# Folding layer 2's column DFT a second time, with the symmetry tests redistributed

## The chip, the cores and the metric

The kernel runs on one core of a Trainium2 chip. The metric is the device time of one execution in microseconds (us), lower is better; a kernel's time is the median of its runs.

The names of the engines: PE is TensorE (matrix products; PEld its weight loads), DVE is VectorE, ACT is ScalarE, POOL is GpSimd, and SP is the sync engine, which here issues nearly all DMAs. Each engine executes its own queue in order.

## The reference

```python
def _A_ref(x, dft_seq_re, dft_seq_im, dft_hid_re, dft_hid_im):
    a = jnp.einsum("bsd,ed->bse", x, dft_hid_re)
    b = jnp.einsum("bsd,ed->bse", x, dft_hid_im)
    return jnp.einsum("ts,bse->bte", dft_seq_re, a) - jnp.einsum("ts,bse->bte", dft_seq_im, b)

def _B_ref(x, w_gate, w_up, w_down):
    h = _sigmoid(jnp.einsum("bsd,df->bsf", x, w_gate)) * jnp.einsum("bsd,df->bsf", x, w_up)
    return jnp.einsum("bsf,fd->bsd", h, w_down)

x = x + _A_ref(_layernorm(x), ...)
x = x + _B_ref(_layernorm(x), ...)
x = x + _A_ref(_layernorm(x), ...)
x = x + _B_ref(_layernorm(x), ...)
```

x has 2048 rows of 640 columns, F is 1728, all float32. The DFT matrices (2048 x 2048 and 640 x 640, real and imaginary) are inputs. `_A_ref` is the real part of a two-dimensional DFT.

## The kernel before

**Numbers.** Float32 operands are split into two float16 parts, and a product is three matmuls: high by high, high by low, low by high (`PASSES`). A split is one ACT instruction (high, L237) and one DVE instruction (low, L239).

**Symmetries.** Cosine and sine rows repeat under t to S - t, S/2 - t, and d to 640 - d. So rows of x are folded in groups GA to GD, columns d with 640 - d: `fold_columns` (L593, L594) makes 321 even sums (EC) and 320 odd differences (EH), `fold_rows` scales and combines (L636 to L642), `fold_join` combines GA with GC (L675) and splits (L677, L682). Whether the input matrices do have these symmetries is tested on the chip while the layers run: a test loads rows or columns of a matrix with DMAs into a "room" of SBUF (L1502, L1519, L1562, L1571), DVE adds or subtracts mirrored parts in place (`test_rows` L1509 and L1511, `test_cols` L1525 to L1528, `test_hidden_rows` L1566, `test_hidden_cols` L1575), and ACT squares and sums the rest (L1481). If the sum is not tiny, a general path runs after the fast one. There are 100 tests and three rooms; a test's load is issued two tests ahead of its check. The list `spans` spreads the tests over the program by weights, 0.4 to 1.1 per unit of PE's time.

**The stages of a layer.** The DFT: `sequence(i, tp)` (L796) multiplies block i of folded rows (four blocks of 128) with the sequence matrix for even (EV) or odd (OD) outputs; `evict_sums` brings the sums from PSUM to SBUF in two halves (L237, L239) as operands z; `hidden(q, ph)` multiplies z with the hidden matrices, `product` (L922) going over three pieces of 128, 128 and 65 rows, for real and imaginary: 18 matmuls of 321 columns into two banks. `hidden_middle` does it for the middle row. `evict_hidden` copies the two banks out: on ACT alone (L971), or for q = 0 one half on ACT (L961) and sum and difference on DVE (L966). `join_hidden` (L996), `add_hidden` (L1009), the row statistics (L424 on DVE, L437 and L438 on ACT), `norm_apply` (L451, L453) and `norm_parts` (L463, L465) make normalized rows, `transpose_pe` (L540) and `transposed` (L550, L552) turn them, and the gate stage starts with `gate_up` (L1130). Later rows are turned by DMA transpositions (`pair_transpose`, L533). The gate stage goes on with `seven` and `four` (L1174: six steps of 54 products of 512 columns in all per column tile j; `snap` L1178 copies a running sum out on ACT between two steps), and the down stage is `stage` (L1430, L1411) or `down` (L1316), with `rows_add` (L1304) on DVE behind each step.

**The order of the work.** Layer 1's DFT follows a list written by hand (`OPENING`). From there, `steps` is the list of PE's work; every other piece of work is put before a step, by `when` (a time on a scale made of the steps' assumed durations) or by `run` (a step's number). A DVE, ACT, POOL or SP instruction therefore stands in its engine's queue at the place where its job comes in this order, and waits there. PSUM has eight banks, which are given out in the order in which they were freed. SBUF is cut into slots whose places are a table (`PLACES`). Layer 2's DFT starts at step `he`: its `order` list names 17 steps, and `run(he + n, ...)` puts the evictions and the row work between them. Its block 3 is joined by the job at `end + 3`, three units into the first step; blocks 0 and 1 are folded during layer 1's second gate stage and spilled, block 2 during its down stage. The split hidden matrices are kept in DRAM from layer 1 (`keep` in `drop_hidden`) and loaded again (`load_wh_again`, L907).

```python
for h in range(2):
    for j in range(0 if h else JC, NF):
        p = seven(j)
        steps += p[:4] + ([four(j - 1)] if j > (0 if h else JC) else []) + p[4:]
```

## Time and profile before

| | us |
|---|---|
| median of 3 runs | 1105.36 |
| lowest, highest | 1103.85, 1106.36 |
| the profiled execution | 1106.03 |
| its span, first to last instruction | 1104.2 |
| PE busy in the span | 1084.0 |
| DVE, ACT, POOL busy | 830.2, 572.9, 154.6 |

On a row of the profile stand the line of the kernel, the engine, the operation, what it writes and reads (`big` is the SBUF tile in which all slots lie, `acc` the PSUM banks), how often, the busy time, and in brackets the idle time of the engine before it with what ended that. The stages on PE by the trace: layer 1's DFT and its first gate products until 154, gate stage 154 to 243, down 243 to 332, gate 332 to 492, down 492 to 572; layer 2's DFT 572 to 612, gate 612 to 780, down 780 to 860, gate 860 to 1018, down to the end.

### The profile page before, as it was taken

The page shows a single profiled execution, that of the slowest core. Times are in us where ns is not written, and L with a number is a line of the kernel's source. Part 1 is how long each engine was busy: PE and PEld are TensorE (multiplying, and loading weights), DVE is VectorE, ACT ScalarE, POOL GpSimd, SP SyncE. Part 2 cuts the span into 40 slices and gives each one's busy share as a digit, 9 for nine tenths or more (in the row PEclk, how much of TensorE's full clock was granted, in tenths as well). Part 3 has the DMA queues.
Part 4 walks back from the last instruction along what each step waited for, and adds up shares of the span by engine and source line. Part 5 has one row for each costly group of instructions (what it writes and reads, how often), then busy time and mean ns, then how long its engine had stood idle before and what let it go on. Part 6 is the DMA issues. An engine that isn't in the chain of part 4 may idle for free.

```text
span 1104.2 us, 17528 instructions
## 1 busy us (share of the span) xinstructions
PE 1084.0 (98%) x6289; PEld 626.3 (57%) x6289; DVE 830.2 (75%) x1608; ACT 572.9 (52%) x1109; POOL 154.6 (14%) x250
## 2 busy tenths in 40 slices
PE   6999999999999999999999999999999999999997
PEld 3776444457774444457777844444677444444775
DVE  8996789868448999769887569895895356777962
ACT  7776547765315665555225544476761345555520
POOL 3110153312333151000110100012000010000010
PEclk9999999999999999999999999999999999999999
DMA  8414765366996877756742058645569856666521
GB/s 273 155 61 71 199 184 203 115 193 191 251 249 233 251 250 202 235 174 214 229 141 73 1 62 194 200 154 182 185 163 177 265 180 208 202 196 194 190 88 64
DMA packets 183079, 194.70 MB, mean 176 GB/s; under 512 B 76451, under 2 KB 145474, under 8 KB 182982
## 3 DMA queue, kind: packets, MB, share of 16 engines
q1 hardware_dynamic: 182342, 190.87, 58.8%
q0 software_dynamic: 640, 2.62, 0.6%
q8 instruction: 51, 0.84, 0.3%
q14 instruction: 46, 0.38, 0.1%
HBM read 145.29 MB, written 31.91 MB: 160 GB/s over the span
## 4 chain that ended last, share of the span: by engine, by line
PE 87%; DVE 8%; issue 2%; DMA 1%; ACT 1%; POOL 0%; SPq 0%; DVEq 0%; POOLq 0%; ACTq 0%
PE acc L1174 36%; PE acc L1430 17%; PE acc L1130 14%; PE acc L1316 8%; PE acc L922 4%; PE acc L1411 2%; PE acc L1283 2%; PE acc L834 2%; DVE big L642 1%; DMA big<-big 1%; DVE quad L424 1%; DVE big L239 1%; PE acc L796 1%; DVE big L1509 1%; DVE big L594 0%
## 5 line engine op out<-in xcount | busy, mean ns | idle before, releaser
L1174 PE MATMUL acc<-big 128*128 128x512 f16 x2160 | 467.8, 379 | 2.8 <-ACT big L1178 1.9
L1174 PEld LDWEIGHTS <-big 128*128 128x128 f16 x2160 | 211.3, 98 | 257.8 <-issue 3.5
L1430 PE MATMUL acc<-big 128*128 128x320 f16 x1512 | 213.2, 299 | 0.4 <-DVE big L1304 0.4
L1178 ACT ACTIVATE big<-acc 128x512 f32<-128x512 f32 x160 | 94.0, 593 | 191.9 <-PE acc L1174 167.5
L1430 PEld LDWEIGHTS <-big 128*128 128x128 f16 x1512 | 147.9, 98 | 58.5 <-issue 0.6
L1130 PE MATMUL acc<-big 128*128 128x512 f16 (+1 forms) x900 | 156.6, 336 | 0.0
L1130 PEld LDWEIGHTS <-big 128*128 128x128 f16 x900 | 87.9, 98 | 67.7 <-DVE big L239 0.2
L1481 ACT ACTIVATE big<-big 128x768 f32<-128x768 f32 (+6 forms) x106 | 79.0, 745 | 53.2 <-DVE big L1511 17.0
L1304 DVE SCALAR_TENSOR_TENSOR big<-acc,big 128x320 f32<-128x320 f32 x112 | 53.1, 485 | 53.7 <-PE acc L1411 27.2
L239 DVE SCALAR_TENSOR_TENSOR big<-big 128x640 f16<-128x640 f32 (+7 forms) x94 | 75.9, 830 | 22.5 <-ACT big L237 19.4
L1316 PE MATMUL acc<-big 128*128 128x320 f16 x656 | 89.3, 299 | 0.0
L1391 DVE TENSOR_TENSOR big<-big 128x512 f16<-128x512 f32 x126 | 85.3, 688 | 2.3 <-ACT big L1390 2.3
L1390 ACT ACTIVATE big<-big 128x512 f16<-128x512 f32 x126 | 74.0, 618 | 25.0 <-DVE big L1391 11.1
L237 ACT ACTIVATE big<-big 128x640 f16<-128x640 f32 (+9 forms) x94 | 63.8, 707 | 35.7 <-POOL big L1082 15.8
L1316 PEld LDWEIGHTS <-big 128*128 128x128 f16 x656 | 64.2, 98 | 25.1
L1224 DVE TENSOR_TENSOR big<-big,acc 128x512 f32<-128x512 f32 x40 | 27.3, 682 | 44.4 <-PE acc L1174 30.6
L516 ACT ACTIVATE big<-big 128x384 f16<-128x384 f32 (+2 forms) x56 | 36.0, 667 | 36.6 <-DVE big L501 17.2
L1181 ACT ACTIVATE big<-big 128x512 f32<-128x512 f32 x80 | 49.7, 622 | 9.7 <-DVE big L1224 6.6
L386 POOL DMA_INDIRECT out<-big,rows x8 | 8.6, 1070 | 310.9 <-DVE big L1304 173.5
L1509 DVE TENSOR_TENSOR big<-big 128x512 f32<-128x512 f32 x64 | 46.2, 722 | 5.9 <-DMA big<-in_ct 5.7
L1402 DVE TENSOR_TENSOR big<-big 128x512 f32<-128x512 f32 x72 | 50.1, 697 | 0.1
L439 POOL TENSOR_SCALAR rowt<-rowt 128x1 f32<-128x1 f32 x24 | 13.0, 540 | 242.4 <-ACT big L437 242.4
(199 smaller groups left out, 1230.2 us busy)
## 6 DMA issues: line engine op xcount, KB each, us to landing
big<-in_ct SPq DMA_DIRECT2D x256, 128.0 KB
big<-kept_f SPq DMA_DIRECT2D x63, 320.0 KB
big<-kept_S SPq DMA_DIRECT2D x33, 512.0 KB
big<-kept_w SPq DMA_DIRECT2D x33, 320.0 KB
big<-in_ct SPq DMA_DIRECT2D x32, 256.0 KB
big<-kept_G SPq DMA_DIRECT2D x21, 320.0 KB
kept_S<-big SPq DMA_DIRECT2D x13, 512.0 KB
big<-in_wg SPq DMA_DIRECT2D x19, 320.0 KB
```

Of the source, the lines that this page charges most:

```text
L237: nc.scalar.activation(dh, src, AF.Copy, scale=s)
L239: nc.vector.scalar_tensor_tensor(dl, src, s, dh, op0=OP.mult, op1=OP.subtract)
L1130: nc.tensor.matmul(ps, w[wp][:, d * P : (d + 1) * P], xt[:, xp, :], start=(d == 0 and wp == HI and xp == HI), stop=(d == ND - 1 and wp == LO))
L1174: nc.tensor.matmul(ps, wt, xt, start=start and n == 0, stop=n == len(todo) - 1, skip_group_check=not start)
L1178: nc.scalar.activation(dst, ps, AF.Copy)
L1304: nc.vector.scalar_tensor_tensor(xe, ps[:, :EH], CB, xe, op0=OP.mult, op1=OP.add)
L1316: nc.tensor.matmul(held["pd", i, e][0][:, :EH], held["t", half, j].parts[hp][:, i * P : (i + 1) * P], held["w", 2, j].parts[wp][:, e * EH ...
L1390: nc.scalar.activation(h, v, AF.Copy)
L1391: nc.vector.tensor_tensor(l, v, h, op=OP.subtract)
L1430: nc.tensor.matmul(ps[:, :EH], a[n][hp][:, i * P : (i + 1) * P], w[n][:, wp], start=fresh and m == 0, stop=m == len(todo) - 1, skip_group_ ...
L1481: nc.scalar.activation(v, v, AF.Square, accum_out=new_sum()[:p])
L1509: nc.vector.tensor_tensor(bd[:, :, 1], bd[:, :, 0], bd[:, :, 1], op=same)
```

## The change

**The second fold.** In layer 2 the 321 even sums and the 320 odd differences are folded again, d with 320 - d: 161 sums and 160 differences each (`fold_again`, four new DVE instructions for a parity pair). Even outputs of the hidden DFT then need only one of the two and odd outputs the other. `product` writes even outputs to the first 161 columns of the bank and odd ones to the next 161; the first two pieces of d have 161 columns each, and the third, with rest rows of both kinds (33 + 32), has 322. So 12 of the 18 matmuls of a `hidden` have half the columns. The evictions put the outputs back in turn: they read the bank with `"p (h k) -> p k h"`. The doubled first column moves to the front of the folded tile. The hidden matrices for layer 2 are loaded raw by `load_wh2` and split by `split_wh2` during layer 1's second down stage, in place of the stores and reloads of the split ones. Scales XF and ZS are halved.

**The order of layer 2's DFT.** `sequence(3, EV)` comes before `sequence(2, OD)`, and both q = 0 steps come together ahead of `sequence(3, OD)`. Block 3 is joined after `evict_sums(0, EV, 0)`, first for EV and, two evictions later, for OD. Products by TensorE, with weight loads between; ahead of them stands the last sequence step. Before:

```order
L796 LDWEIGHTS big
L796 MATMUL acc_312<-big 65x256
L922 LDWEIGHTS big
L922 MATMUL acc_315<-big 128x321
L922 LDWEIGHTS big
L922 MATMUL acc_315<-big 128x321
```

After, at the fifth product of `hidden(0, 0)`:

```order
L976 LDWEIGHTS big
L976 MATMUL acc_327<-big 128x161
L976 LDWEIGHTS big
L976 MATMUL acc_327<-big 128x161
L976 LDWEIGHTS big
L976 MATMUL acc_327<-big 128x322
L976 LDWEIGHTS big
```

Where nine products of 321 columns went into a bank, six of 161 do, and then three of 322.

DVE's queue at the start of layer 2's DFT, from the end of block 3's `fold_rows`. Before (L675 and L682 are `fold_join`, L239 is an eviction, L966 is `evict_hidden`):

```order
L642 SCALAR_TENSOR_TENSOR big<-big,quad_77 128x320
L675 TENSOR_TENSOR big<-big 128x321 x2
L675 TENSOR_TENSOR big<-big 128x320 x2
L682 TENSOR_TENSOR big<-big 128x2x321
L682 TENSOR_TENSOR big<-big 128x2x320
L239 SCALAR_TENSOR_TENSOR big<-acc_314,big 128x512
```

After (L699 and L708 are `fold_join`, L684 is `fold_again`, L241 an eviction):

```order
L656 SCALAR_TENSOR_TENSOR big<-big,quad_78 128x320
L241 SCALAR_TENSOR_TENSOR big<-acc_326,big 128x512
L699 TENSOR_TENSOR big<-big 128x321 x2
L699 TENSOR_TENSOR big<-big 128x320 x2
L684 TENSOR_TENSOR big<-big 128x161
L684 TENSOR_TENSOR big<-big 128x160
L684 TENSOR_TENSOR big<-big 128x161
L684 TENSOR_TENSOR big<-big 128x160
L708 TENSOR_TENSOR big<-big 128x321 x2
L241 SCALAR_TENSOR_TENSOR big<-acc_66,big 128x512
```

An eviction moved ahead of the join, and four instructions came in between join and split; the other two evictions, four more second folds and the splits of the OD half follow.

**The tests.** Six tests of the second fold's symmetry are new (`test_hidden_fold`), 106 in all. The weights in `spans` are new; the hidden tests get a room of their own and one test more of time between load and check. By DVE's rows, layer 1's second down stage has 5 tests after 9, layer 2's first gate stage 27 after 24 (with `gate_up`), its first down stage 4 after 6, its last gate stage 49 after 33, and its last down stage 5 after 5. SP's queue in layer 2's last gate stage, between two loads of a `kept_S` weight (L1104 before, L1167 after). Before:

```order
L1104 DMA big<-kept_S_2853 128x2048
L1109 DMA big<-kept_w_4_1115 128x2x384
L1502 DMA big<-in_ct 128x1x256 x8
L1103 DMA big<-kept_w_5_1151 128x1280
L1104 DMA big<-kept_S_2936 128x2048
```

After:

```order
L1167 DMA big<-kept_S_2868 128x2048
L1172 DMA big<-kept_w_4_1115 128x2x384
L1565 DMA big<-in_ct 128x1x256 x12
L1625 DMA big<-in_wh 128x1x320 x2
L1565 DMA big<-in_ct 128x1x256 x4
L1166 DMA big<-kept_w_5_1151 128x1280
L1167 DMA big<-kept_S_2951 128x2048
```

Eighteen loads of tests stand between the weights where eight stood.

**Else.** Layer 2's rows for the second half are prepared at 6, 18, 42 and 51 units of its first down stage instead of 6, 20, 46 and 56. At the start eleven small DVE instructions make the scales `hs2` behind `hs`. The slots are placed anew. The diff, cut to its core:

```diff
-XF = 2.0**8
+XF = 2.0**7
...
+    hs2 = pool.tile([P, 5], F32, name="hs2")
...
+        p = part[:, 34:35]
+        nc.vector.tensor_scalar(hs2[:, 0:1], p, 1.0, 0.5 * CS, op0=OP.is_ge, op1=OP.mult)
+        nc.vector.tensor_scalar(hs2[:, 0:1], hs2[:, 0:1], 0.5 * CS, None, op0=OP.add)
+        for k, op, a, b in ((1, OP.is_le, 31, 32), (2, OP.is_ge, 33, 34), (3, OP.is_le, 30, 31), (4, OP.is_ge, 33, 33)):
+            for c, v in ((hs2[:, k : k + 1], a), (part[:, 36 + k : 37 + k], b)):
+                nc.vector.tensor_scalar(c, p, float(v), 0.5 * CS, op0=op, op1=OP.mult)
+        nc.vector.tensor_tensor(hs2[:, 1:5], hs2[:, 1:5], part[:, 37:41], op=OP.add)
...
+    def fold_again(to, f, r):
+
+        c, every = EH - 2 * r, (slice(None),) * (len(f.shape) - 1)
+        for n, to_c, op in ((HE + 1, 0, OP.add), (HE, HE + 1, OP.subtract)):
+            nc.vector.tensor_tensor(to[(*every, slice(to_c, to_c + n))], f[(*every, slice(0, n))],
+                                    f[(*every, slice(c, c - n, -1))], op=op)
...
             if 1 in do:
-                nc.scalar.activation(take_parts(key, i)[:, :, 0, :w], f[:, GB::2], AF.Copy)
-                if n:
-                    nc.gpsimd.memset(take_parts(key, i)[:, :, :, EH : EH + 1], 0.0)
+                fold_again(a, b, n)
             if 2 in do:
-                p = take_parts(key, i)
-                nc.vector.tensor_tensor(p[:, :, 1, :w], f[:, GB::2], p[:, :, 0, :w], op=OP.subtract)
-                folded_at[fold, i] = True
+                nc.scalar.activation(p[:, :, 0, :EC], a, AF.Copy)
+            if 3 in do:
+                nc.vector.tensor_tensor(p[:, :, 1, :EC], a, p[:, :, 0, :EC], op=OP.subtract)
...
     def product(ps, ph, r, at, m):
-        for d, (_, n) in enumerate(KT[r]):
-            w = held["h", r, d].f16[:n]
+        for d, (_, n) in enumerate(KT):
+            o = ps[:m, : EC + 1 if steps else EC]
+            if steps and d < 2:
+                c = (r + d) % 2
+                o = ps[:m, c * (HE + 1) : (c + 1) * (HE + 1)]
+            ws = [w[:n, : o.shape[1]] for w in held["h", r, d].parts]
...
-                    nc.tensor.matmul(ps[:m, :EC], z[:, at : at + m], w[:, 384 * wp : 384 * wp + EC],
+                    nc.tensor.matmul(o, z[:, at : at + m], ws[wp],
...
+    def sums_of_bank(ps):
+        return ps[:, : EC + 1].rearrange("p (h k) -> p k h", h=2) if steps else ps[:, :EC]
+
+    def in_order(v):
+        return v.rearrange("p (k h) -> p k h", h=2) if steps else v[:, :EC]
...
-                nc.scalar.activation(v[:, n], ps[:, :EC], AF.Copy, scale=CY)
+                nc.scalar.activation(in_order(v[:, n]), sums_of_bank(ps), AF.Copy, scale=CY)
...
-                     (sequence, 2, OD), (hidden, 0, 0), (sequence, 3, EV), (hidden, 1, 0), (sequence, 3, OD),
-                     (hidden, 0, 1), (hidden, 2, 0), (hidden, 3, 0), (hidden, 1, 1), (hidden, 2, 1), (hidden, 3, 1),
-                     (hidden_middle,)]
+                     (sequence, 3, EV), (sequence, 2, OD), (hidden, 0, 0), (hidden, 0, 1), (sequence, 3, OD),
+                     (hidden, 1, 0), (hidden, 1, 1), (hidden, 2, 0), (hidden, 3, 0), (hidden_middle,),
+                     (hidden, 2, 1), (hidden, 3, 1)]
...
-            u = d0 + ((2, 20, 47, 57) if first else (6, 20, 46, 56))[i]
+            u = d0 + ((2, 20, 47, 57) if first else (6, 18, 42, 51))[i]
...
-    spans = [(start_of(0, "d", 0) + 6, start_of(0, "d", 0) + 38, 0.4), (start_of(0, "d", 0) + 76, start_of(0, "e"), 0.55),
...
+    spans = [(d[0] + 6, d[0] + 38, 0.5), (d[0] + 76, d[1] - 43, 0.12), (d[1] - 43, d[1] - 3, 0.7), (d[1] - 3, d[1] + 57, 0.3),
+             (c - 11, j, 0.8), (j, d2 - 28, 0.6), (d2 - 28, d2 - 4, 0.8), (d2 + 6, d2 + 38, 0.35), (j2, j2 + 23, 0.5),
+             (j2 + 23, j2 + 63, 1.4), (j2 + 63, e2, 1.1), (e2, e2 + 25, 0.6)]
```

184 lines of the change are left out of this document (118 added, 66 removed), and 64 rows, old and new, of the table PLACES.

## The prediction

> **What bounds the kernel now.** I read the page's first part, then the waits of PE, then the time line of PE, DVE and ACT around layer 2's transform, and the table by windows. Page:
>
> ```profile
> span 1104.2 us, 17528 instructions
> PE 1084.0 (98%) x6289; PEld 626.3 (57%) x6289; DVE 830.2 (75%) x1608; ACT 572.9 (52%) x1109; POOL 154.6 (14%) x250
> ```
>
> PE is the bound: 20 us of the span are without a matmul. The waits of PE that the change can reach (total, times, longest):
>
> ```profile
> PE acc L1174 <- ACT big L1178: 1.9, 1, 1.9
> PE acc L1174 <- DMA big<-big: 0.9, 1, 0.9
> PE acc L796 <- DVE big L239: 0.6, 1, 0.6
> PE acc L922 <- ACT big L971: 0.5, 1, 0.5
> ```
>
> So PE work removed is worth its full time, if the engines that feed PE keep up. The stage that the change rebuilds, on PE's time line (start, us, instruction, count):
>
> ```profile
> 571.66 2.47 PE L796 MATMUL acc<-big 128*128 128x257 f16 x21
> ...
> 581.90 2.78 PE L796 MATMUL acc<-big 128*65 128x256 f16 x24 [0.56 <-DVE big L239]
> ...
> 610.00 2.63 PE L922 MATMUL acc<-big 128*97 128x321 f16 x18 [0.53 <-ACT big L971]
> 612.46 6.71 PE L1130 MATMUL acc<-big 128*128 128x256 f16 x60
> ```
>
> It lasts from 571.66 to 612.46, 40.8 us, with two waits of 1.1 together. The chain in order of time gives paces without the drain of the last matmul:
>
> ```profile
> 584.68 2.46 PE acc L922 x18
> ...
> 619.18 1.12 PE acc L540 x20
> ...
> 691.78 79.64 PE acc L1174 x369
> ```
>
> A product of 321 columns takes 137 ns, a 128-column transposition 56, a 512-column product 216. These lie on one line of 0.417 ns a column plus 2.6 ns.
>
> **Removed from PE.** Of the 18 products of each `hidden`, 12 go from 321 to 161 (or 161 with a zero column) columns, 6 go to 322. By the line 161 columns take 69.7 ns, so one `hidden` takes 12 x 0.0697 + 6 x 0.137 = 1.66 instead of 2.46. Nine of them (eight and the middle one) give **-7.3 us**. The 8 `sequence` steps keep their shapes. The pace rests on weight loads hiding behind short products. The loads of the transpositions (line, shape, count, busy, mean ns, idle):
>
> ```profile
> L540 PEld LDWEIGHTS <-big 128*128 128x128 f16 x80 | 4.9, 98 | 0.3
> ```
>
> Each is busy for 98 ns, and yet 20 transpositions, each with a load of its own, come at 56 ns: loads overlap at 128 columns already. The Trainium skill (TensorE: Matmul & The Clock Gate, section "Back-to-back issue gap") says of streams of load and product that 128 columns take about 81 ns. By that figure, put beside the line's slope, the short products would take about 95 ns and the term would be -4.5; the row of 56 ns speaks against it.
>
> **New waits in the same stage.** PE's stage shortens, the vector work in it grows. The rows of DVE:
>
> ```profile
> 550.53 0.49 DVE L1511 TENSOR_TENSOR big<-big 128x128 f32<-128x128 f32 x2
> ...
> 576.90 1.02 DVE L642 SCALAR_TENSOR_TENSOR big<-big,quad 128x321 f32<-128x321 f32 x2 [0.79 <-ACT big L636]
> 577.84 1.69 DVE L675 TENSOR_TENSOR big<-big 128x321 f32<-128x321 f32 x4
> 579.60 1.65 DVE L682 TENSOR_TENSOR big<-big 128x642 f16<-128x642 f32 x2
> 581.16 3.67 DVE L239 SCALAR_TENSOR_TENSOR big<-acc,big 128x512 f16<-128x512 f32 x6
> ...
> 596.52 0.89 DVE L966 SCALAR_TENSOR_TENSOR big<-acc,big 128x321 f32<-128x321 f32 x2 [1.63 <-ACT big L961]
> 597.45 0.83 DVE L996 TENSOR_TENSOR big<-big 128x642 f32<-128x642 f32 x1
> 598.31 1.56 DVE L1009 TENSOR_TENSOR big<-big 128x642 f32<-128x642 f32 x2
> 599.79 0.88 DVE L424 BATCH_NORM_STATS2 rowt<-big 128x6 f32<-128x320 f32 x2
> ...
> 605.97 0.56 DVE L453 TENSOR_SCALAR big<-big,rowt 128x640 f32<-128x640 f32 x1
> 606.45 1.71 DVE L465 TENSOR_TENSOR big<-big 128x640 f16<-128x640 f32 x2
> ```
>
> and of ACT:
>
> ```profile
> 580.29 2.99 ACT L237 ACTIVATE big<-acc 128x512 f16<-128x512 f32 x6
> ...
> 601.65 1.40 ACT L971 ACTIVATE big<-acc 128x321 f32<-128x321 f32 x4
> 603.58 0.92 ACT L451 ACTIVATE big<-big,rowt 128x640 f32<-128x640 f32 x1 [0.53 <-DVE rowt L414]
> 604.53 0.74 ACT L463 ACTIVATE big<-big 128x640 f16<-128x640 f32 x1
> ...
> 608.70 0.83 ACT L438 ACTIVATE big<-big,rowt 128x640 f32<-128x640 f32 x1
> ...
> 610.16 1.30 ACT L550 ACTIVATE big<-acc 128x640 f16<-128x640 f16 x2
> ```
>
> Each second fold is four 160-column instructions per parity; between the 128-column 0.25 and the 321-column 0.42 I take 0.25. I follow the new order on the old clock. Block 3's rows are done at 577.9 as now (that hangs on PE's last rows, unchanged). DVE then: one eviction 0.6, four joins 1.7, four second folds 1.0 (581.2), halves split with ACT between, 1.0: the even inputs are ready at 582.2. PE, no longer held by a bank, wants `sequence(3, EV)` at 582.0: wait 0.25. DVE goes on without a gap: two evictions 1.2, folds 1.0, splits 0.9, then the odd evictions, the first done at 586.0, where PE wants its bank at 585.5 (`sequence(2, OD)`, last third): 0.5. The six evictions end at 589.05; `hidden(0, 1)` needs the last of them at 588.7: 0.35. That step ends at 590.3. Then the row chain: differences by 591.65, join 0.8, additions 1.6, statistics 1.1, join 0.8 to 596.0; ACT's two passes over row 1, 0.83 each at most, from 594.1; the (1, OD) evictions stand behind them and start at 596.6. `hidden(2, 0)` needs their first bank: PE at 596.4, bank at 597.2: 0.8. ACT evicts four `hidden` at 0.35 a half, 597.6 to 600.4, normalizes row 0 (0.92 and 0.74) and row 1, DVE splits both by 604.05; PE asks for them at 603.0 and its 20 transpositions end 0.2 late. ACT then has row 3's two passes before it evicts `hidden(2, 1)`, whose banks `hidden(3, 1)` takes: 0.9. Sum 3.0 instead of 1.1, so **+1.9**; the stage takes 35.4 us. Cover behind it is enough: rows 2 and 3 are asked for only after two more `gate_up`, 6.6 us later. If the evictions' interleaved reads cost double, that is rival 2.
>
> **Elsewhere.** The wait of 1.9 follows a stretch in which DVE has no slack; by windows (us, PE, PEld, DVE, ACT, POOL busy):
>
> ```profile
> 360.00:432.00 72.00, 70.10 (x326) 31.71 (x325) 71.42 (x122) 44.59 (x80) 22.39 (x27) 1.00 0.74 235
> 860.00:1018.00 158.00, 157.93 (x732) 71.61 (x732) 99.22 (x192) 78.14 (x161) 4.19 (x4) 1.00 0.63 205
> ```
> ```profile
> 360.00:432.00 72.00, 6.75 (x9) 1.00 0.74 235
> ```
>
> The second fence is line 1509 alone: nine row tests here, 0.75 and two of about 0.25 each. With the new weights (0.12 for 0.55) some two remain: 8.5 us less for DVE, against 4 instructions of second fold for each of blocks 0 and 1 (3.3 us at twice 160 columns). DVE is 5 us freer, the wait goes: **-1.9**. The 0.9 is a transposition that lands late:
>
> ```profile
> 850.82 7.16 SPq L533 DMA_TRANSPOSE big<-big  x1
> ```
>
> Its row is prepared 5 us earlier now, and two row tests fewer stand beside it: **-0.9** (0 if SP is what holds it). Splitting the hidden matrix again (8 short instructions on ACT and on DVE, about 2.2 us each, 8 loads for 6) lies in layer 1's last stage, which loses four tests, 4.7 us of DVE; without that cover it would cost at most its 2.2. The stores of the six split matrices on SP's queue go. Opening:
>
> ```profile
> 4.81 0.15 DVE L315 TENSOR_SCALAR hs<-hs 128x1 f32<-128x1 f32 x1
> ...
> 7.48 0.83 DVE L593 TENSOR_TENSOR big<-big 128x640 f32<-128x640 f32 x1 [1.48 <-ACT big L363]
> ```
>
> Eleven more instructions like the first are 1.7 us at 0.15 each, against 1.48 of idle time ahead of the next step that counts: 0 to 0.2, and I take 0. In layer 2's last gate stage 49 tests stand instead of 33 (counted in the order of DVE's rows):
>
> ```profile
> L1502 SPq DMA_DIRECT2D big<-in_ct x256: 588/597/2972, 251.6 to 989.2; - x128
> ```
> ```profile
> 913.55 0.43 SPq L1107 DMA_DIRECT2D big<-kept_U  x1
> ```
> ```profile
> DVE big L1509 <- DMA big<-in_ct: 4.4, 5, 2.2
> ```
>
> A test's load takes SP 0.6, a weight load 0.43, three to a step. Where 18 loads of tests stand in a step, SP needs 10.8 and 1.3, and PE's 54 products of 216 ns take 11.65: SP falls behind by 0.4 there and catches up after. DVE has 59 us idle in that window, the 16 tests ask about 15. I charge 0.5 (bounds 0 and 12, rival 3). **Sum**: -7.3 + 1.9 - 1.9 - 0.9 + 0.5 = -7.7. The profiled execution took 1106.03 (1.8 around its span), the median of the runs 1105.36; the gain taken from the median gives **1097.7**.
>
> **Rivals.** (1) The short products don't do what they say: weight loads, 98 ns each, set the pace. 108 products at 98 instead of 69.7 ns give back 3.1: 1100.8. The 56 ns of the transpositions speak against it, though they load from rows of one tile and these from z. The Trainium skill's pair rate, named above, is this case. (2) The evictions read even and odd halves in turn, 644 bytes apart in PSUM; no row shows such a read. If it doubles, ACT's eight halves cost 2.8 more ahead of row 0 and DVE's four differences 1.8 more ahead of that; less the slack of 0.2 the transpositions come 4.4 later: 1102.1. For it: this chain is what PE waits for. Against: strided DVE reads of SBUF (line 1511, every second column) go at full rate. The Trainium skill (SBUF — State Buffer, section "Door 1: The DMA port swizzle") says that PSUM has lines of 8 bytes and that non-contiguous access slows matmuls much; no run here shows it. (3) **Slower**: the dense tests in layer 2's last gate stage. DVE waits in order for a load, ACT's square waits for DVE, and behind it stands the copy of `chain`, which PE needs 15 products (3.2 us) later; 0.6 of that is the copy. It decides once DVE waits over 2.6 us; today's longest is 2.2. If 24 row tests come 0.5 past that, PE loses 12: 1109. For it: SP is full there; against: such waits reach PE nowhere in this window today. (4) Better: no new wait, all four old ones gone: -7.3 - 1.1 - 2.8 = -11.2: 1094.2.
>
> **Chances.** Forecast 0.56 (1095.5 to 1100), rival 1 0.06, 2 0.13, 4 0.10, 3 in full 0.08, in part or with 2 so that nothing measurable is left 0.07. Within 0.2% (2.2 us, about what a measurement of this kernel can tell from no change): 0.07; slower 0.08; faster 0.85. The range 1094.0 to 1103.0 leaves out rival 3, the case of no change and a tail of rivals 2 and 4.
>
> **What would show it.** Right: products of 161 columns at about 70 ns; the stage from first L796 product to first `gate_up` near 35.4 us, with waits for `fold_join`'s splits, the evictions and the rows; no wait over 0.5 at layer 1's gate stages. Wrong: evictions over 0.45 a half (rival 2), short products over 80 ns (rival 1), PE waiting for ACT's copies after 880 (rival 3).

## The result, and the profile after

The changed kernel took **4225.85 us** (median of 4 runs, 4222.53 to 4227.57) beside 1105.26 before: a ratio of 3.8233 [3.8167, 3.8299]. The forecast was 1097.7 us. Two things went wrong, and they are of very different size. The page of the kernel after, its first part and two of its costliest groups:

```profile
span 4225.8 us, 36649 instructions
PE 4054.4 (96%) x14321; PEld 2141.3 (51%) x14321; DVE 1145.3 (27%) x2303; ACT 679.7 (16%) x1403; POOL 247.7 (6%) x640
...
L2141 PE MATMUL acc<-big 128*128 128x512 f32 x2560 | 1103.0, 594 | 23.6 <-DMA big<-in_ct 19.3
L2188 PE MATMUL acc<-big 128*128 128x512 f32 (+1 forms) x2240 | 979.1, 600 | 3.0 <-ACT big L2175 3.0
```

36649 instructions where before had 17528, and 14321 matmuls for 6289: no wait explains that, something runs that did not run before. The two groups are float32 products in `general`. The time line of the kernel after shows where it begins (start, us, instruction, count):

```profile
1138.95 0.84 PE L1474 MATMUL acc<-big 128*128 128x320 f16 x5
...
1141.46 8.84 SPq L2126 DMA_DIRECT2D big<-in_x  x14
```

The fast path's last products end at 1139.8. At 1141.46 the general path loads x again, and it runs to 4225.8: 3084 us. So the guard on the symmetries, which rests on the sum of the tests, failed. That is the first thing. The second: the fast path's last products should have ended 8 us before those of the kernel before, which end at 1097.5 on its trace, and ended 42 us behind them.

Inside the fast path, the rebuilt stage does what was forecast. PE's time line from layer 2's first `sequence` products to its first `gate_up`:

```profile
567.09 2.46 PE L825 MATMUL acc<-big 128*128 128x257 f16 x21
...
581.49 0.81 PE L825 MATMUL acc<-big 128*65 128x256 f16 x6 [0.79 <-DVE big L241]
582.14 3.50 PE L976 MATMUL acc<-big 128*128 128x161 f16 x36
585.47 2.13 PE L825 MATMUL acc<-big 128*128 128x256 f16 x18
...
592.57 6.00 PE L976 MATMUL acc<-big 128*128 128x161 f16 x63 [0.81 <-DVE big L241]
...
600.18 1.83 PE L976 MATMUL acc<-big 128*128 128x161 f16 x18 [0.50 <-ACT big L1032]
601.85 6.72 PE L1193 MATMUL acc<-big 128*128 128x256 f16 x60
```

567.09 to 601.85 is 34.8 us, where before took 40.8. The 36 products of two `hidden` steps fill 582.14 to 585.47, 1.66 us a step. Three waits are left, 2.1 in all. PE's waits that are new are elsewhere (total, times, longest):

```profile
PE acc L1237 <- ACT big L1241: 31.4, 13, 4.5
PE acc L1237 <- DMA big<-kept_G: 4.1, 1, 4.1
```

L1237 are the gate stages' products, L1241 is the copy `snap`; before had this wait once, 1.9. The table by windows, over layer 2's last gate stage (us, then busy and instructions of PE, PEld, DVE, ACT, POOL, then PE's clock, DMA share, GB/s):

```profile
862.00:1018.00 156.00, 129.56 (x550) 55.84 (x549) 78.33 (x165) 64.87 (x142) 4.21 (x4) 0.93 0.53 173
```

Every engine does less here than before, when PE was full, and the DMA engines move less too, 173 GB/s for 203 in the same window. On the average of the window nothing is full: PE stands in a chain of waits.

### The profile page after: what moved, and what is told of

Its sections match the earlier page's. It is cut to its first block, busy times and chain, and to the rows that moved or that the text cites. A ratio compares the mean times of both kernels' runs of the same rounds, so it can differ in the third digit from the quotient of the medians.

```text
span 4225.8 us, 36649 instructions
## 1 busy us (share of the span) xinstructions
PE 4054.4 (96%) x14321; PEld 2141.3 (51%) x14321; DVE 1145.3 (27%) x2303; ACT 679.7 (16%) x1403; POOL 247.7 (6%) x640
## 5 line engine op out<-in xcount | busy, mean ns | idle before, releaser
L2141 PE MATMUL acc<-big 128*128 128x512 f32 x2560 | 1103.0, 594 | 23.6 <-DMA big<-in_ct 19.3
L2188 PE MATMUL acc<-big 128*128 128x512 f32 (+1 forms) x2240 | 979.1, 600 | 3.0 <-ACT big L2175 3.0
L2141 PEld LDWEIGHTS acc<-big 128*128 128x128 f32 x2560 | 487.8, 191 | 638.0 <-issue 612.4
L2188 PEld LDWEIGHTS acc<-big 128*128 128x128 f32 (+1 forms) x2240 | 421.5, 189 | 556.1 <-issue 550.6
L1237 PE MATMUL acc<-big 128*128 128x512 f16 x2160 | 483.2, 386 | 37.5 <-ACT big L1241 31.4
L2196 PE MATMUL acc<-big 128*128 128x320 f32 (+1 forms) x1792 | 495.4, 436 | 0.0
L2196 PEld LDWEIGHTS acc<-big 128*128 128x128 f32 (+1 forms) x1792 | 334.9, 190 | 163.0 <-issue 31.0
L1237 PEld LDWEIGHTS <-big 128*128 128x128 f16 x2160 | 214.2, 99 | 305.1 <-issue 55.5
L2155 PE MATMUL acc<-big 128*128 128x320 f32 x1280 | 344.9, 432 | 0.0
L2190 DVE TENSOR_TENSOR big<-acc,big 128x512 f32<-128x512 f32 x112 | 77.4, 691 | 922.6 <-PE acc L2188 922.6
L2155 PEld LDWEIGHTS acc<-big 128*128 128x128 f32 x1280 | 243.2, 190 | 102.0 <-issue 1.0
L2123 DVE TENSOR_TENSOR big<-acc,big 128x320 f32<-128x320 f32 x128 | 62.9, 492 | 774.0 <-PE acc L2196 459.8
L1493 PE MATMUL acc<-big 128*128 128x320 f16 x1512 | 213.4, 299 | 0.4 <-DVE big L1367 0.4
L2189 ACT ACTIVATE big<-acc 128x512 f32<-128x512 f32 x112 | 66.9, 597 | 883.3 <-PE acc L2188 883.3
L1241 ACT ACTIVATE big<-acc 128x512 f32<-128x512 f32 x160 | 93.0, 591 | 165.8 <-PE acc L1237 163.0
```

The source lines that it names most:

```text
L1237: nc.tensor.matmul(ps, wt, xt, start=start and n == 0, stop=n == len(todo) - 1, skip_group_check=not start)
L1241: nc.scalar.activation(dst, ps, AF.Copy)
L1493: nc.tensor.matmul(ps[:, :EH], a[n][hp][:, i * P : (i + 1) * P], w[n][:, wp], start=fresh and m == 0, stop=m == len(todo) - 1, skip_group_ ...
L2123: nc.vector.tensor_tensor(xe, p, xe, op=OP.add)
L2141: nc.tensor.matmul(acc[d // 2][d % 2], xn[i][:, d * P : (d + 1) * P], c, start=i == 0, stop=i == NS - 1)
L2155: nc.tensor.matmul(ps[e][:, :EH], z[r][d][:, i * P : (i + 1) * P], h[r][d][:, e * EH : (e + 1) * EH], start=r == 0 and d == 0, stop=r == 1 ...
```

## The experiments

The times are medians (of one run where "single run" is said) against the kernel before on the same chip, which took 1103.7 to 1105.0 there. In each kernel the table of slots (`PLACES`) is laid out anew beside the edit shown; what that alone can do is seen under "Other spreads". The stages are lengths on PE by the trace; "first gate" is layer 2's with its `gate_up`, "last gate" its second one.

| kernel | us | ratio [95%] | layer 1 down | layer 1 gate 2 | DFT 2 | first gate | down | last gate |
|---|---|---|---|---|---|---|---|---|
| before | 1105.26 | | 89.1 | 160.1 | 40.8 | 167.2 | 80.4 | 158.0 |
| after | 4225.85 | 3.8233 | 89.1 | 158.0 | 34.8 | 177.3 | 79.3 | 201.2 |
| rooms_apart | 1149.04 | 1.0395 [1.0378, 1.0413] | 89.1 | 158.0 | 34.7 | 178.5 | 79.3 | 198.8 |
| reversed | 4226.47 | single run | | | | | | |
| no_tests | 1097.26 | 0.9933 [0.9918, 0.9948] | 89.1 | 158.0 | 34.8 | 167.2 | 79.3 | 158.0 |
| old_spread | 1115.47 | 1.0097 [1.0081, 1.0114] | 89.1 | 174.3 | 35.7 | 167.2 | 80.3 | 158.0 |
| before_dense | 1150.47 | 1.0401 [1.0384, 1.0418] | 91.8 | 159.6 | 40.8 | 177.3 | 79.3 | 191.3 |
| one_load | 1112.68 | single run | 89.2 | 157.9 | 34.8 | 168.6 | 79.3 | 170.0 |
| four_small | 1115.14 | single run | 89.1 | 158.0 | 34.7 | 172.2 | 79.4 | 170.8 |
| pool_loads | 1148.34 | single run | 89.1 | 158.0 | 34.7 | 178.0 | 80.3 | 197.5 |
| five_rooms | 1140.44 | single run | 89.0 | 158.0 | 34.8 | 176.6 | 79.4 | 189.7 |
| five_pool | 1142.92 | single run | 89.1 | 158.0 | 34.7 | 176.4 | 80.2 | 189.2 |
| spread | 1115.81 | 1.0111 [1.0094, 1.0128] | 89.4 | 164.5 | 34.8 | 167.2 | 81.1 | 168.9 |
| three_flat | 1130.56 | 1.0229 [1.0214, 1.0245] | 89.2 | 157.9 | 34.8 | 175.4 | 87.1 | 177.7 |
| five_flat | 1131.33 | 1.0233 [1.0218, 1.0248] | 92.8 | 160.8 | 34.7 | 178.0 | 85.2 | 169.8 |
| tuned | 1136.48 | 1.0286 [1.0262, 1.0310] | 92.9 | 160.9 | 34.7 | 174.4 | 85.7 | 169.6 |
| tuned_three | 1130.54 | 1.0239 [1.0223, 1.0256] | 89.2 | 157.9 | 34.8 | 174.0 | 82.4 | 181.5 |
| even | 1119.44 | 1.0128 [1.0111, 1.0145] | 89.5 | 162.6 | 34.7 | 172.5 | 82.9 | 169.1 |
| early | 1118.51 | 1.0123 [1.0101, 1.0145] | 100.6 | 160.8 | 34.7 | 168.3 | 80.0 | 158.0 |
| downs | 1120.78 | 1.0143 [1.0120, 1.0166] | 106.5 | 159.6 | 34.8 | 168.5 | 80.4 | 158.0 |

### Why the general path ran

The lines of the change that place the hidden tests, which the core of the diff left out:

```python
    for n, test in enumerate(more):
        tests.insert(30 + 4 * n, test)
...
    slow = [n for n, test in enumerate(tests) if test in more]
...
        k, late = (3, 1.0) if n in slow else ((n - sum(m < n for m in slow)) % 3, 0)
        when(at_test(n), within, k, load, *key)
        when(at_test(n + 2 + late), within, k, test, *key)
```

`insert` is asked for the places 30, 34, ... 114. But with 84 other tests the list is only 102 long when the last four are put in, so they land at its end, side by side, in places 102 to 105. All use room 3, and a test there is checked three tests after its load. The kernel after's time line, SP's queue with the last six loads of hidden columns, and then DVE with their checks:

```profile
1034.65 0.34 SPq L1649 DMA_DIRECT2D big<-in_wh  x1
1047.04 0.33 SPq L1649 DMA_DIRECT2D big<-in_wh  x1
1065.99 0.35 SPq L1649 DMA_DIRECT2D big<-in_wh  x1
1068.69 0.33 SPq L1649 DMA_DIRECT2D big<-in_wh  x1
1073.49 15.54 SPq L1649 DMA_DIRECT2D big<-in_wh  x2
...
1045.08 0.81 DVE L1653 TENSOR_REDUCE cmax<-big 128x1 f32<-128x640 f32 x1
...
1059.94 0.81 DVE L1653 TENSOR_REDUCE cmax<-big 128x1 f32<-128x640 f32 x1
...
1087.34 0.80 DVE L1653 TENSOR_REDUCE cmax<-big 65x1 f32<-65x640 f32 x1
...
1093.16 0.81 DVE L1653 TENSOR_REDUCE cmax<-big 128x1 f32<-128x640 f32 x1
1098.25 0.81 DVE L1653 TENSOR_REDUCE cmax<-big 128x1 f32<-128x640 f32 x1
...
1102.71 0.81 DVE L1653 TENSOR_REDUCE cmax<-big 65x1 f32<-65x640 f32 x1
```

Load, check, load, check goes well twice. The third load (1065.99) is checked at 1087.34; the fourth and fifth went into the same room at 1068.69 and 1073.49. The check reads another test's columns. The sixth load, held until this check, follows at 1088.7, and the checks behind it read the room as that load and the earlier checks left it. Nothing in the program's order is violated: the loads stand ahead of the check in it. Theory A: this overwriting alone raises the flag. Its rival: one of the tests itself, the new ones of the second fold above all, does not hold for these inputs.

**rooms_apart** leaves the order as it is and gives the last three tests the other rooms; room 3 is given up at the end.

```diff
-    slow = [n for n, test in enumerate(tests) if test in more]
+    slow = [n for n, test in enumerate(tests) if test in more][:-3]
...
-    when(at_test(slow[-1] + 3.9), drop, "room", 3)
+    when(at_test(len(tests) + 2.9), drop, "room", 3)
```

> The last three of the hidden tests, which stand side by side at the end of the list, use the first three rooms instead of the fourth; nothing else changes. Theory A (the four last tests share one room, so a load overwrites what an earlier test was to check, the sum of rests is not tiny and the general path runs): the general path, 3086 us from 1139.8 to 4225.8 in the trace, goes, and the kernel ends where its fast path ended: about 1143 us. Rival B (the second fold's symmetry, or one of its six new tests, fails by itself): still 4226 us.

1149.04, 6 above what was expected. No general path, with every one of the 106 tests still made; so the tests hold, and the rival falls. The price of the overwriting is 4225.85 - 1149.04 = 3076.8. What is left, 44 us above before, is the second thing.

**reversed** puts the hidden tests in from the other end of their list, so that others collide.

```diff
-    for n, test in enumerate(more):
+    for n, test in enumerate(more[::-1]):
```

> The changed kernel with the 22 hidden tests in the opposite order, so that four tests of hidden rows, which also stand in the kernel before, are the last instead of the tests of hidden columns. Theory A (it is the place at the end of the list): the general path runs again, 4226 us. Rival C (the hidden tests of columns are broken by their new room, wherever they stand): also 4226 if C, but with the place filled by tests of rows, A and C differ only if the first two theories are mixed; a time near 1143 us would make C false and A false as well, and would leave the tests' kind at the end as the cause.

4226.47: the collision, not a particular test, raises the flag. From here on, all kernels build on rooms_apart, but for no_tests, which builds on the kernel after, and before_dense.

### The fold or the tests

**no_tests** leaves out all 106 tests, and the two of the matrices' edges that stand beside them (and never takes the general path). **old_spread** has the weights of before, **before_dense** is the kernel before with the weights of after.

```diff
-    for n, (load, test, key) in enumerate(tests):
-        k, late = (3, 1.0) if n in slow else ((n - sum(m < n for m in slow)) % 3, 0)
-        when(at_test(n), within, k, load, *key)
-        when(at_test(n + 2 + late), within, k, test, *key)
-        when(at_test(n + 2.85 + late), square_rest)
```

> The changed kernel with all tests of the symmetries left out and the general path never taken: what the second fold gives without them. By the stages of rooms_apart that no test disturbs: 1105 less 6.1 (layer 2's DFT), 2.1 (layer 1's second gate stage), 0.4 and 1.1 (down stages): 1095 us, and 1 to 2 less as the tests' loads and sums are gone elsewhere too.

```diff
-             (j2 + 23, j2 + 63, 1.4), (j2 + 63, e2, 1.1), (e2, e2 + 25, 0.6)]
...
+             (start_of(1, "j", 1, 0), start_of(1, "j", 1, 0) + 50, 0.6),
+             (start_of(1, "j", 1, 0) + 50, start_of(1, "d", 1), 1.1), (start_of(1, "d", 1), start_of(1, "d", 1) + 30, 0.6)]
```

> As rooms_apart, with the list of spans and weights of the kernel before (weights 0.4 to 1.1 in place of 0.12 to 1.4); the second fold, the 106 tests and the fourth room stay. Theory D (the dense tests hold DVE and ACT in layer 2's two gate stages, 10 us in the first and 43 us in the last): nearly all of these 53 us go, except that layer 1's second gate stage has its wait of 1.9 back: 1105 - 6.0 (layer 2's DFT stage as measured) - 1 to - 4 elsewhere, 1095 to 1099 us. Rival E (the fourth room and the later check of its tests hold SP's queue, at any weights): 1115 us or more.

In before_dense the same two lists change places, in the other kernel.

> The kernel before with the new spans and weights alone: 100 tests, three rooms, no second fold. Theory D: the waits come with the weights, so layer 2's gate stages lose most of 53 us, somewhat less as there are 6 tests fewer: 1135 to 1155 us. Rival E (fourth room) or a cause in the second fold: 1103 to 1107 us.

no_tests: 1097.26, 2 above the 1095 expected, with every gate stage at the length of full PE, 167.2 (with `gate_up`) and 158.0. old_spread: 1115.47, where theory D missed by 16 and rival E's time came; layer 2's waits are gone, its last gate stage is back at 158.0, but 14 us come up in layer 1's second gate stage. PE's waits in old_spread, and the first of them on the time line:

```profile
PE acc L1237 <- ACT big L1241: 11.3, 4, 4.7
```
```profile
390.20 36.81 PE L1237 MATMUL acc<-big 128*128 128x512 f16 x162 [4.75 <-ACT big L1241]
```

The two longest of these four waits, 4.75 and 4.14, have another chain than layer 2's: ACT itself waited 9.21 and 8.15 just before, until a store on SP's queue had landed (`kept_e`, a folded block, 8.7 after its issue, and `kept_f`, a split weight, 7.5). The waits of ACT for `kept_e` come back in spread (7.3) and even (7.8); the kernel before has one of 2.4 in that stage, no_tests none. So neither the old tests without the fold nor the fold without tests brings them, but the two together. Which part does it was not run apart: the second fold's work ahead of the store, the six new tests, the fourth room and its later checks as in rival E, or the places of the slots.

before_dense: 1150.47, with PE's waits

```profile
PE acc L1174 <- ACT big L1178: 24.3, 9, 6.1
PE acc L1174 <- DMA big<-kept_G: 3.9, 2, 3.5
```

So the kernel before, without the second fold, loses 45 us by the new weights alone. For layer 2's waits the second fold is not needed.

How one such wait comes about is seen around 904 in the kernel after. SP, DVE, ACT and PE on its time line:

```profile
890.50 13.13 SPq L1565 DMA_DIRECT2D big<-in_ct  x12
...
903.12 0.69 DVE L1572 TENSOR_TENSOR big<-big 128x512 f32<-128x512 f32 x1 [5.50 <-DMA big<-in_ct]
...
904.42 0.85 ACT L1544 ACTIVATE big<-big 128x768 f32<-128x768 f32 x1 [6.21 <-DMA big<-in_ct]
...
905.26 0.58 ACT L1241 ACTIVATE big<-acc 128x512 f32<-128x512 f32 x1
...
905.89 14.28 PE L1237 MATMUL acc<-big 128*128 128x512 f16 x53 [4.45 <-ACT big L1241]
```

Twelve loads take SP 13.13 us, 1.09 each with the waits between them. DVE's row test (L1572) waits 5.50 for its load, ACT's square (L1544) stands behind that, the copy of the running sum (L1241) stands behind the square, and PE waits 4.45 for the copy. In rooms_apart DVE's wait of this kind and PE's, by the waits of the last gate stage:

```profile
DVE big L1572 <- DMA big<-in_ct: 42.9, 18, 5.6
...
PE acc L1237 <- ACT big L1241: 28.7, 12, 4.3
```

The stage is 40.8 longer; 28.7 of that are waits, and 9.9 are 48 products at half pace after six of the waits (by PE's start times; see the last section). The rest, some 2, lies at the edges of the twelve waits.

### What in a test's load is late

A row test (`load_rows`) issues four loads of 128 KB on SP's queue. Theory F: their number is what counts; theory G: their bytes. **one_load** brings the same bytes in one DMA, **four_small** a quarter of the bytes in four, **pool_loads** issues half of layer 2's loads on POOL's queue. The first two load other data than a test needs (four_small also scales the square, so that the sum stays finite), and never take the general path.

```diff
-        s = 1 + 16 * k
-        for g, (row, d) in enumerate(((s, 1), (S - s, -1), (HS - s, -1), (HS + s, 1))):
-            nc.sync.dma_start(v[:, g], bass.AP(ct.tensor, (r * S + row) * S, [[256, 8], [d * S, 16], [1, 256]]))
+        s = 1 + P * (k // 8)
+        nc.sync.dma_start(v, bass.AP(ct.tensor, (r * S + s) * S + 64 * (k % 8), [[S, P], [400, 4], [1, 256]]))
```

> As rooms_apart, but a test of rows loads its 512 pieces of 1 KB with one DMA instead of four (rows one below the other, so the test checks something else), and the general path is never taken. Theory F (SP's issue, 0.6 us for each of the four loads, sets the pace of the dense tests): a row test costs SP 0.6 to 1 us instead of 2.4, and the waits in layer 2's gate stages, 52 us in all with the slow restarts, go: 1095 to 1105 us. Rival G (the bytes: 0.5 MB for each test beside the weights): as rooms_apart, 1149 us.

```diff
-            nc.sync.dma_start(v[:, g], bass.AP(ct.tensor, (r * S + row) * S, [[256, 8], [d * S, 16], [1, 256]]))
+            nc.sync.dma_start(v[:, g, :64], bass.AP(ct.tensor, (r * S + row) * S, [[256, 8], [d * S, 16], [1, 64]]))
```

> As rooms_apart, but each of the four loads of a row test moves 64 of the 256 columns, so a quarter of the bytes in as many pieces; the test then looks at stale columns too, its squares are scaled down, and the general path is never taken. Theory F (SP's issue of four loads): still 1140 to 1150 us. Rival G (the bytes): 1095 to 1110 us.

```diff
-            nc.sync.dma_start(v[:, g], bass.AP(ct.tensor, (r * S + row) * S, [[256, 8], [d * S, 16], [1, 256]]))
+            (nc.gpsimd if r == 1 and g % 2 else nc.sync).dma_start(v[:, g], bass.AP(ct.tensor, (r * S + row) * S, [[256, 8], [d * S, 16], [1, 256]]))
```

> As rooms_apart, but two of the four loads of each row test of the sine matrix, which are the row tests of layer 2's last gate stage, are issued by POOL instead of SP; POOL is busy there for 4 of 158 us. Theory F (SP's issue): half the issue time of these tests leaves SP, and most of the 41 us of the last gate stage go, while the first one keeps its 11: 1105 to 1120 us. Rival G (bytes): about 1149 us, or more if POOL's issue is slow.

1112.68, 1115.14 and 1148.34; the first two lie between what F and what G would give, the third where G has it. Neither theory stands alone: a quarter of the DMAs and a quarter of the bytes each bring the last gate stage from 198.8 to 170 or 171, and another queue brings 1. The windows of that stretch, first rooms_apart:

```profile
862.00:1018.00 156.00, 130.54 (x561) 56.70 (x560) 79.95 (x169) 65.89 (x144) 4.32 (x4) 0.95 0.54 177
```

one_load:

```profile
862.00:1018.00 156.00, 149.15 (x669) 66.27 (x668) 103.71 (x221) 82.80 (x179) 4.21 (x4) 0.97 0.71 225
```

four_small:

```profile
862.00:1018.00 156.00, 146.62 (x665) 65.54 (x663) 102.80 (x218) 82.15 (x179) 4.21 (x4) 0.98 0.53 161
```

one_load moves 225 GB/s, more than any other kernel here, so the rate of bytes is not the limit. What both share is that a test holds the queue for less time; that this is what helps is argued. The longest of SP's own waits for its row loads in rooms_apart's last gate stage shows with what the queue is held:

```profile
SPq L1565 <- DMA big<-in_wh: 11.8, 7, 3.2
```

SP waits to issue until loads that it issued earlier have landed. Before its row loads all waits of this kind come to 21.2 us there, in the kernel before to 2.5. The longest in the kernel before is for ACT's squares, which free a room:

```profile
SPq L1502 <- ACT big L1481: 10.1, 6, 2.6
```

Each DMA of SP signals one of eight semaphores in turn, and so waits for the one eight before it. Worked out from the semaphore events of the traces: all eight were in flight for 0.11 of the last gate stage before, 0.44 in rooms_apart, 0.04 in one_load and 0.15 in four_small, and a row load landed after a median of 5.4, 6.4, 8.1 (four times the size) and 3.1 us. That agrees with a limit of landing time times number in flight. But old_spread, by the same working, has all eight in flight for 0.41 of its last gate stage, with a median landing of 6.4, and no wait of PE there. So a full queue alone does not make the waits; how many loads are asked for counts as well, and the next section's runs do not settle it either.

### More rooms

Theory H: the rooms are too few, a room being held from issue to square. **five_rooms** has five rooms for the row and column tests from layer 2's last gate stage on, and checks two tests later there.

```diff
-        k, late = (3, 1.0) if n in slow else ((n - sum(m < n for m in slow)) % 3, 0)
+        k, late = (3, 1.0) if n in slow else (fast(n) % 3, 0) if n < n0 else ((0, 1, 2, 4, 5)[(fast(n) - fast(n0)) % 5], 2.0)
```

> As rooms_apart, with the weights of the change, but from layer 2's last gate stage on the row and column tests have five rooms and a load is issued four tests ahead of its check instead of two. Theory H (what counts is the time from load to check: two tests at 2.5 to 3.2 us are 5.0 to 6.4 us, less than the four loads' issue of 2.4 and a landing of some 4 to 6.5 us; SP's issue and the bytes count only as parts of that time): four tests are 10 to 13 us, most of the 41 us of the last gate stage go, the 11 of the first gate stage stay: 1108 to 1116 us. Rival I (SP or the DMA queue simply has too much to do there): 1140 to 1150 us.

1140.44: 8.6 of the 44 us, in the range of rival I, so H is a small part at most; 1.9 of it came in layer 2's first gate stage, ahead of the fifth room. **five_pool** has the edits of five_rooms and of pool_loads together: if rooms and queue are each half the limit, both at once must show it.

> As rooms_apart with its dense weights, with both remedies in layer 2's last gate stage: five rooms and a lead of four tests (alone 1140 us, the stage 189.7 us), and half the loads of the row tests issued by POOL (alone 1148 us, the stage 197.5). In the program each of SP's DMAs waits for the one issued eight earlier to have landed, whatever it loaded. Theory J (two limits of nearly the same height: three rooms, each busy from its load to its square, and eight DMAs of SP in flight; removing one leaves the other): the stage falls by more than the two gains of 9.1 and 1.3 together, to 165 to 178 us, and the kernel to 1115 to 1128. Rival K (neither is the limit; the queue of bytes in the DMA engines is): about 187 to 190 us, 1138 to 1142.

1142.92, no better than five_rooms; theory J fails, and rival K's stage of 187 to 190 is met with 189.2. POOL's loads are not slower to land. From the source view of the row loads in pool_loads, POOL's alone:

```profile
DMA to landing us min/median/max: 3.9/6.5/7.7
```

SP's took a median of 6.4 in rooms_apart. But the half that stayed on SP's queue in pool_loads took 9.0, by the semaphore events as above: the second queue's loads came at the cost of the first's. Why is not shown.

### Other spreads

If it is density, another spread should bring the gain of no_tests. In these lists `per(a, b, s)` asks for one test in s units of the scale on which work is placed, up to the common pace; `d` are the starts of layer 1's two down stages (`d[0] + 76` is near the start of its second gate stage), `c` and `j` of layer 2's first `gate_up` and of its first gate steps, `g0` of layer 1's first gate steps, `d2`, `j2` and `e2` of layer 2's first down stage, its last gate stage and its last down stage. **spread**, on rooms_apart:

```diff
+    spans = [per(d[0] + 6, d[0] + 38, 6.0), per(d[0] + 76, d[1] - 43, 14.0), per(d[1] - 43, d[1] - 3, 5.0), per(d[1] - 3, d[1] + 57, 9.0),
+             per(c + 5, j, 6.0), per(j, d2 - 7, 4.1), per(d2 + 6, d2 + 58, 7.0), per(j2, j2 + 23, 5.5),
+             per(j2 + 23, e2, 3.85), per(e2, e2 + 35, 5.5)]
```

> As rooms_apart (second fold, 106 tests, four rooms), with a flatter spread: a test every 14 us of PE's planned time in the first part of layer 1's second gate stage (29 in rooms_apart, 7.6 in old_spread), every 4.1 and 3.85 in layer 2's two gate stages (2.5 to 5.8 in rooms_apart). Theory D (only tests closer than about 3.8 us hold PE): no wait over 1 us in layer 2's gate stages, layer 1's second gate stage at most 2 us longer than 158: the kernel before less 6.1 (layer 2's DFT), 1 to 2 (gate stage of layer 1) and 1 (the late transposition): 1096 to 1098 us. Rival E (the fourth room holds SP at any spread): 1105 us or more.

**three_flat** makes the gate stages even, and **five_flat** the same with five_rooms' rooms:

```diff
+    spans = [per(d[0] + 6, d[0] + 38, 7.0), per(d[0] + 76, d[1] - 43, 29.0), per(d[1] - 43, d[1] - 3, 5.0), per(d[1] - 3, d[1] + 57, 11.6),
+             per(c + 5, j, 6.0), per(j, d2 - 7, 3.6), per(d2 + 6, d2 + 58, 7.0), per(j2, j2 + 23, 5.0), per(j2 + 23, e2, 3.6), per(e2, e2 + 35, 5.5)]
```

> The same flat spread with three rooms and a lead of two tests (7.2 us). Theory H: about the needed time from load to check, so some waits as in spread (where a spacing of 3.85, 7.7 us of lead, cost 11 us in the last gate stage): 1105 to 1115 us. Rival I: the same time as five_flat.

> Five rooms as in five_rooms, and a flatter spread: layer 1 as in the change (22 tests), layer 2's gate stages a test every 3.6 us, none before the first gate stage's weights are asked for. Theory H: a lead of 14 us in the last stage, 7.2 in the first one: no wait over 1 us but in the first; the kernel before less 6.1, 2.1, 1.1 and 0.4: 1094 to 1099 us. Rival I: as three_flat.

**tuned_three** changes the second line of that, **tuned** the same with five_pool's rooms and queue:

```diff
-             per(c + 5, j, 6.0), per(j, d2 - 7, 3.6), per(d2 + 6, d2 + 58, 7.0), per(j2, j2 + 23, 5.0), per(j2 + 23, e2, 3.6), per(e2, e2 + 35, 5.5)]
+             per(c + 5, j, 6.0), per(j, d2 - 7, 4.2), per(d2 + 6, d2 + 58, 6.0), per(j2, e2, 3.82), per(e2, e2 + 45, 5.0)]
```

> The spread of tuned with three rooms and all loads on SP: what the two remedies are worth at a moderate density. Theory J (three rooms: about 3.6 us of cycle for each test, so 3.82 is just above it; old_spread paid nothing at 3.82, spread 11 us at 3.85): 1100 to 1112 us.

> Five rooms and POOL's loads as in five_pool, and a spread that takes from each earlier run the densest setting that cost nothing: layer 1 as in the change (22 tests), layer 2's first gate stage a test every 4.2 us as in old_spread, its last gate stage every 3.82. Theory J: no wait over 1 us in layer 2's gate stages: no_tests' 1097 plus 0 to 4: 1097 to 1101 us, and faster than the kernel before by 0.4 to 0.7%. Rival K: as three_flat or spread, 1108 to 1118.

**early** begins in layer 1's first gate stage, **downs** puts more into layer 1's first down stage, both with 7.0 for the first 50 units of the last gate stage and 3.82 behind; **even** has 4.2 throughout it:

```diff
+    spans = [per(g0 + 6, d[0] - 10, 9.0), per(d[0] + 6, d[0] + 38, 6.0), per(d[0] + 38, d[0] + 76, 12.0), per(d[0] + 76, d[1] - 43, 29.0),
+             per(d[1] - 43, d[1] - 3, 5.0), per(d[1] - 3, d[1] + 57, 11.6), per(c + 5, j, 6.0), per(j, d2 - 7, 4.2),
+             per(d2 + 6, d2 + 58, 9.3), per(j2, j2 + 50, 7.0), per(j2 + 50, e2, 3.82), per(e2, e2 + 35, 6.5)]
```

> As rooms_apart (three rooms and the fourth), with a spread that leaves layer 2 as in old_spread, which had no wait there: 35 tests before layer 2's gate stages, of which 8 already in layer 1's first gate stage, one every 9 us, and few in the first part of layer 1's second gate stage, where old_spread lost 14 us. Theory K (tests cost nothing where eight DMAs of SP are rarely in flight at once, whatever their number in all): no wait over 1 us behind the opening, the 1097 us of no_tests plus 0 to 4: 1097 to 1101. If layer 1's first gate stage has no room for them (DVE is busy for 71.6 of 89 us there): 1105 to 1115.

```diff
+    spans = [per(d[0] + 4, d[0] + 76, 5.6), per(d[0] + 76, d[1] - 43, 29.0), per(d[1] - 43, d[1] - 3, 4.6), per(d[1] - 3, d[1] + 57, 9.0),
+             per(c + 5, j, 6.0), per(j, d2 - 7, 4.2),
+             per(d2 + 6, d2 + 58, 9.3), per(j2, j2 + 50, 7.0), per(j2 + 50, e2, 3.82), per(e2, e2 + 35, 6.5)]
```

> As early, but the tests that layer 1's gate stages don't take stand in its first down stage, one every 5.6 us over 72 us (one every 7 over 32 us in the change), where DVE is busy for 54 of 89 us but the DMA engines already for 0.83 of the time. Theory K: the DMA side is what the tests need, so this is the worse place: 1102 to 1115 us; if DVE's time is what they need, 1097 to 1101.

```diff
+    spans = [per(d[0] + 6, d[0] + 38, 6.0), per(d[0] + 76, d[1] - 43, 24.0), per(d[1] - 43, d[1] - 3, 5.0), per(d[1] - 3, d[1] + 57, 9.0),
+             per(c + 5, j, 6.0), per(j, d2 - 7, 4.2), per(d2 + 6, d2 + 58, 7.0), per(j2, e2, 4.2), per(e2, e2 + 48, 5.0)]
```

> The last spread, with three rooms and the fourth: none of the places that cost something in an earlier run (layer 1's first gate stage and the end of its first down stage, which made a weight late by 11 and 17 us; spacings under 4.2 in layer 2), 25 tests in layer 1, layer 2's gate stages one every 4.2 us throughout, more in its last down stage. Theory K: below the density that holds PE: 1098 to 1104 us, faster than the kernel before. If the place of the row tests (four DMAs each) in the last gate stage matters more than the mean spacing, as tuned_three (23 us lost at 3.82) against old_spread (none at 3.82) suggests: 1105 to 1115.

In none of the eight did the leading theory's time come: 1115.8, 1130.6, 1131.3, 1130.5, 1136.5, 1118.5, 1120.8 and 1119.4 are all above before, and in each the loss moved to where the tests went. three_flat and five_flat took the same time, as rival I has it. But SP, DVE and ACT have the same instructions in the same order in these two up to 881 us, and only the table of slots differs; still layer 1's two stages took 92.8 and 160.8 in five_flat for 89.2 and 157.9. PE waits 3.5 there for a `kept_S` weight, issued behind a DMA transposition (L542) at 324.5, which stands at 316.5 in three_flat. tuned and tuned_three are apart in the same way. So the places of the slots alone can cost 6.5 us, and differences of a few us between the spreads are not the spread's for certain. spread took what rival E has (1105 or more), and that rival was not run by itself. early and downs are the plainest. Their last gate stage has no wait at all, but one weight load of layer 1's second gate stage came late behind the tests of its down stage; early:

```profile
349.98 152.51 PE L1237 MATMUL acc<-big 128*128 128x512 f16 x693 [11.07 <-DMA big<-kept_w]
```

downs:

```profile
349.02 151.37 PE L1237 MATMUL acc<-big 128*128 128x512 f16 x693 [17.25 <-DMA big<-kept_w]
```

early lost another 7.2 in layer 1's first gate stage (95.3 for 88.1), which has no column in the table.

No version with all tests beat the kernel before.

**What stays open.** Which quantity sets the limit (landing time and eight in flight, or something in the DMA engines that shortens with fewer bytes and with fewer DMAs alike) is not settled: five_rooms should have been helped by neither and was by 8.6, and old_spread's queue was nearly as full as rooms_apart's at no cost. What brings the 14 us into layer 1's second gate stage in old_spread is open too, and no two spreads were run with the slots in the same places. Nor is why one test in 3.82 units costs nothing in the second part of the stage in early, and some 23 us over the whole of it in tuned_three. A row test that makes the full test with fewer DMAs was not run.

## Why the prediction was wrong

**Whether the fast path is the program that runs.** The step that failed first is one that the sum lacks: it adds up terms of the fast path alone, and so puts the general path at nothing without a reason. Behind that stands the sentence "the hidden tests get a room of their own and one test more of time between load and check", which the account of the change passes on and which the prediction never priced: four tests at the end of the list share that room. Its rival 1, "the short products don't do what they say", asks this of the products; none asks it of the tests: that the flag is raised and 3077 us follow. The order of SP's queue, written out, would have shown six loads of L1649 against the checks that belong to them. rooms_apart and reversed show this cause.

**The dense tests.** "I charge 0.5 (bounds 0 and 12, rival 3)". They cost 43.2 in the last gate stage (201.2 for 158.0) and 10.1 in layer 2's first (177.3 for 167.2), 53 us in all. The mechanism is rival 3's word for word, DVE in order for a load, the square, the copy, PE; the size failed, at three places. First, "A test's load takes SP 0.6": that is an instruction's own time. In a burst a load takes 1.09 (12 in 13.13), and 18 of them 19.7 us, where PE's step takes 11.65. Over the whole stage the 104 row loads took 102.1, 0.98 each. So SP doesn't fall behind by 0.4 and catch up, it stays behind. The time line of the kernel before could have said so:

```profile
914.56 8.48 SPq L1502 DMA_DIRECT2D big<-in_ct  x8
```

1.06 a load there too, and 1.04 over all 80 row loads of that stage (83.0 us), the waits for free rooms within it; eight of them fit a step, eighteen at that pace (19.1) don't. As the rooms are part of that pace, it was a warning and not a price. Second, "DVE has 59 us idle in that window" is an average: DVE takes its work in order, so its idle time becomes waits of up to 5.6 while the tests are late. Third, the bound of 12 took 0.5 for each row test; the twelve waits of PE in rooms_apart are 2.4 on average, and after six of them products come at half pace, which the prediction had no term for. The 4.1 for kept_G in the first gate stage was not looked for at all.

**The products, -7.3: right.** 1.66 a step, and the stage at 34.8 for a forecast of 35.4. Rival 1 (98 ns for each of the short ones, 24 in two steps, and 137 for the 12 others) would be 4.0 for two steps where 3.33 stand.

**New waits, +1.9: right in kind, a little high.** The waits are 0.8, 0.8 and 0.5, 2.1 where 3.0 were summed: three of the six that were worked out, and the other three did not come. The one of 0.8 for `hidden(2, 0)` was met exactly. Rival 2 falls by the source view of the kernel after, ACT's evictions:

```profile
L1032 ACT ACTIVATE big<-acc x24: 418/440/474, 61.9 to 602.0; 128x321 f32<-128x321 f32 x12, 128x322 f32<-128x322 f32 x12
```

and the same line of before, where none is interleaved:

```profile
L971 ACT ACTIVATE big<-acc x24: 417/430/448, 63.8 to 615.1; 128x321 f32<-128x321 f32 x24
```

The median mixes layer 1's twelve, which read in order, with layer 2's twelve; by form, the twelve that read the two halves of a bank in turn (322 columns) average 447 ns, and those of before 431. 16 ns each is far from the double that rival 2 asks for. Rival 4 asked for all waits to go; 2.1 us of them stayed.

**The two waits elsewhere, -1.9 and -0.9: right.** Layer 1's second gate stage went from 160.1 to 158.0, layer 2's first down stage from 80.4 to 79.3. The ground of the first was thinner than summed, though: DVE was to be 5 us freer from 360 to 432, and is busy for 69.7 in rooms_apart where before had 71.4. Of the second's two grounds each was enough: the wait for the transposition is gone in old_spread, with the earlier rows alone, and in before_dense, with the fewer tests alone. Splitting the hidden matrix again in layer 1's second down stage cost nothing (79.9 before, 79.5 after), and so did the scales in the opening.

**The sum without tests.** no_tests, at 1097.26, comes close to the 1097.7; but it leaves work out that before has, and before was not run without its tests. It confirms the terms stage by stage, not the total. With all tests kept, the fold's gain was outweighed in every spread that was run: in old_spread by the 14.2 us that came up in layer 1's second gate stage, against 5.1 won in the DFT.
